# Trading the two row tiles of TensorE: one runs the first matmul of its tokens while the other runs output rounds

## The chip, the cores and the metric

One core of one Trainium2 chip. Times are device microseconds of whole executions; most executions of one kernel agree within 0.3%. A ratio is the mean time of one kernel's runs over that of the other's of the same rounds, so not quite the ratio of the medians that are quoted.

## The reference

A causal convolution of 7 taps per head (8 heads of 24 channels, weights through a softmax) over 32768 tokens of 192 channels, then a two-layer network with ELU between:

```python
out = einsum('hk,bskhg->bshg', softmax(weight), windows(x))     # 192 channels
h = out @ w_in                                                  # 192 -> 2048
g = where(h > 0, h, exp(min(h, 0)) - 1)
return g @ w_out                                                # 2048 -> 192
```

## The kernel before

The contraction of each matmul is 64 rows long, so TensorE works as two **row tiles** of 64 rows. Tokens come in super-tiles of 1024, and each tile has one **group** of 512 tokens for the first matmul. A **step** n is one slice of 128 of the 2048 hidden columns, for both groups:

- PE: three matmuls of 512 columns per tile (64 channels each) into one of three PSUM **slots** `H`, each slot with one bank per group.
- ACT: `E = exp(H)`, one instruction per group. POOL: clamps `E` to at most 1. DVE: `gT = max(E - 1, H)`. Only when DVE has read `H` is the slot free.
- PE again, one super-tile later: the second matmul. A **round** is one matmul of 192 columns on each tile. 64 rounds make one output **half** in the accumulator `ops` (two banks, one only for each group), and ACT copies it to `osb`. After 32 rounds the two tiles swap banks.

Eight steps belong to one output half. I number them 0 to 7: steps 0 to 6 hold 10, 10, 6, 6, 10, 11, 11 rounds, step 7 none, so that the copy of the accumulator has time. In step 5 a convolution of a later super-tile runs too, in two parts; it takes one slot as well, and ACT copies it to `csb`.

```python
HALF_STEPS = (10, 10, 6, 6, 10, 11, 11)
...
# PE: one step = the pair of groups, then its rounds (with convolution parts in between in step 5)
elif item[0] == "h":
    ...
    wait_slot(k)                              # s_tt >= 2*was+2: DVE is done with both groups
    for j in range(3):
        for r in range(2):                    # tile 0, tile 1
            ins = pe.matmul(H[:, k % 3, GS*r : GS*(r+1)], w_in[...], att[...],
                            start=(j == 0), stop=(j == 2), tile_position=(HP * r, 0))
    ins.then_inc(s_h)                         # one count for both groups
else:
    _, t, half, r0, r1 = item
    if r0 == 0: W(s_oev, 2 * t + half)        # the copy of the half before must be done
    for r in range(r0, r1):
        ...
        for rt in range(2):
            g = rt ^ second                   # banks swap after 32 rounds
            ins = pe.matmul(acc[:, g, D*kb : D*(kb+1)], gT[...], w_out[...],
                            tile_position=(HP * rt, 0))
    if r1 == NR: ins.then_inc(s_mm2)

# ACT, in the same order of items
if item[0] == "c": ...  W(s_cv, 2*m + 2);  csb <- H            # convolution's copy
elif item[0] == "h": W(s_h, n + 1); ...    E <- exp(H), twice  # both groups
else: if r1 == NR: evac(t, half)                               # osb <- ops, 128x768
```

Of the kernel before, what the change touches and what calls it, by code (L numbers as in the profile page):

```python
# [12 lines left out]
P = 128  # L13
HP = 64
FC = 128
D = 192
# [19 lines left out]
HALF_STEPS = (10, 10, 6, 6, 10, 11, 11)  # L36
# [8 lines left out]
def bass_lightweight_conv__then__act_elu_kernel(  # L45
# [26 lines left out]
    steps = []  # L72
# [9 lines left out]
    order = []  # L82
    last_half = (NS - 1, 1)
# [13 lines left out]
    for t in range(NS):  # L97
        base = NQ * (t + 1) + LAG
        for half in range(2):
            r = 0  # L100
            for i, cnt in enumerate(HALF_STEPS):
                rounds_at[base + 8 * half + i] = (t, half, r, r + cnt)
                r += cnt
            assert r == NR
    for n in range(NP + NQ + LAG):
# [8 lines left out]
        convs = [(k, u) for k, u in convs if k < NS]  # L114
        if n in rounds_at:
            t, half, r0, r1 = rounds_at[n]
            if (t, half) == last_half and r0 == 0:
                last_slot = take_slot(None)
            cuts = (r0, r0 + 3, r0 + 7, r1) if convs else (r0, r1)
            for part, (a, b) in enumerate(zip(cuts, cuts[1:])):  # L120
                order.append(("o", t, half, a, b))
                for k, u in convs:
                    if part < 2:
                        conv_at(k, u, part)
        else:
            for k, u in convs:
                for part in range(2):
                    conv_at(k, u, part)

# [3 lines left out]
    with ExitStack() as stack:  # L133
# [110 lines left out]
        def transpose(eng, W, s):  # L244
# [3 lines left out]
            if s >= 2:  # L248
                W(s_h, NQ * (s - 1))
# [6 lines left out]
        def _gpsimd(g: bass.BassGpSimd):  # L256
# [56 lines left out]
            for n in range(NP):  # L313
# [12 lines left out]
                for u in range(2):  # L326
                    W(s_exp, 2 * n + u + 1)
# [10 lines left out]
        def _scalar(a):  # L338
# [26 lines left out]
            for item in order:  # L365
# [6 lines left out]
                elif item[0] == "h":  # L372
                    n = item[1]
                    k = slot_of_pair[n] % 3
                    W(s_h, n + 1)
                    W(s_tt, 2 * (n - NE) + 2)
                    for u in range(2):
                        a.activation(  # L378
                            E[:, n % NE, u, :], H[:, k, GS * u : GS * (u + 1)], ACT.Exp
                        ).then_inc(s_exp)  # L380
# [6 lines left out]
        def _vector(v):  # L387
# [27 lines left out]
            for n in range(NP):  # L415
# [3 lines left out]
                for u in range(2):  # L419
                    W(s_clp, 2 * n + u + 1)  # L420
# [17 lines left out]
        def _tensor(pe):  # L438
            W = Waits(pe)

            def wait_slot(k):
# [3 lines left out]
                if was[0] == "h":  # L445
                    W(s_tt, 2 * was[1] + 2)
# [8 lines left out]
            warm(WARM[0])  # L455
            for item in order:
                if item[0] == "c":
                    _, m, part = item
                    s, u = divmod(m, 2)
                    k = slot_of_conv[m]  # L460
# [9 lines left out]
                    else:  # L470
                        if 2 <= m <= 3:
                            warm(WARM[2])
                        W(s_cswap, 2 * m + 2)

                    for q in range(2):
                        for rt in range(2):
                            hq = 2 * (rt ^ part) + q
                            h = HU * u + hq
                            rows = slice(HP * rt, HP + (KW - HP) * rt)
                            ins = pe.matmul(  # L480
                                H[0:CW, k % 3, 256 * hq : 256 * hq + UC],
                                Tm[rows, h, :] if s else Tk[rows, :, h],
                                xg[rows, s % NXB, :, CPH * h : CPH * (h + 1)].rearrange(
                                    "p w (j i) -> p j w i", j=3
                                ),
                                start=(part == 0 and q == 0),
                                stop=(part == 1 and q == 1),
                                tile_position=(HP * rt, 0),
                            )
                            if q == 1 and part == 0:  # L490
                                ins.then_inc(s_cswap)
                            elif q == 1:
                                ins.then_inc(s_cv)
                elif item[0] == "h":
                    n = item[1]
                    s, q = divmod(n, NQ)
                    if n == 0:
                        warm(WARM[1])
                    elif n < NQ - 1:
                        warm(WARM[2])  # L500
                    W(s_w[q // QA], 48)
                    W(s_wdp if q < QA else s_wd[1], 16)
                    W(s_att[s % 2], 16 * (s // 2 + 1))
                    k = slot_of_pair[n]
                    wait_slot(k)
                    for j in range(3):
                        for r in range(2):
                            ins = pe.matmul(  # L508
                                H[:, k % 3, GS * r : GS * (r + 1)],
                                w_in[HP * r : HP * (r + 1), j, FC * q : FC * (q + 1)],  # L510
                                att[HP * r : HP * (r + 1), s % 2, j, 0:GS],
                                start=(j == 0),
                                stop=(j == 2),
                                tile_position=(HP * r, 0),
                            )
                    ins.then_inc(s_h)
                else:
                    _, t, half, r0, r1 = item
                    W(s_w[2], 16)
                    if (t, half) == last_half:  # L520
                        acc = H[:, last_slot % 3, :].rearrange("p (g t) -> p g t", g=2)
                        if r0 == 0:
                            wait_slot(last_slot)
                    else:
                        acc = ops
                        if r0 == 0:
                            W(s_oev, 2 * t + half)
                    for r in range(r0, r1):

                        second, (q, kb) = r // (NR // 2), divmod(r % (NR // 2), 2)  # L530
                        W(s_tt, 2 * (NQ * t + q) + 2)
                        if second:
                            W(s_swap, 2 * (2 * t + half + 1))
                        t0 = 2 * P * half + P * kb
                        for rt in range(2):
                            g = rt ^ second
                            ins = pe.matmul(  # L537
                                acc[:, g, D * kb : D * (kb + 1)],
                                gT[HP * rt : HP * (rt + 1), t % NG3, q, g, t0 : t0 + P],
                                w_out[HP * rt : HP * (rt + 1), q, :],  # L540
                                start=(r == 0),
                                stop=(r == NR - 1),
                                tile_position=(HP * rt, 0),
                            )
                            if r == NR // 2 - 1:
                                ins.then_inc(s_swap)
                    if r1 == NR:
                        ins.then_inc(s_mm2)
# [79 lines left out]
```

## Time and profile before

Before: 758.62 us median of 4 runs (757.49 to 760.06).

The page of the kernel before: busy time and share of the span by engine, then the chain that ended last.

```profile
PE 746.0 (99%) x11872; PEld 510.7 (68%) x11872; DVE 636.0 (84%) x1033; ACT 645.8 (85%) x1155; POOL 668.3 (88%) x1110
...
PE 94%; DVE 2%; DMA 2%; POOL 1%; ACT 1%; issue 0%; SPq 0%
```

PE is never idle for long. Start to start in the trace, two first matmuls side by side take 216 ns, a round 82.5 ns, two convolution matmuls 102.5 ns. One half is then 24 x 216 + 64 x 82.5 + 4 x 102.5 ns = 10.87 us of TensorE work; the trace repeats every 11.19 us. So 0.32 us per half, 20 us in the run, are stalls.

The timeline of PE in the kernel before, around the end of one half (start, length in us, group, count): step 5 with its convolution, step 6 (0.82 + 1.07), then the pairs of steps 7 and 0 as one group of 12, then the first rounds of the next half.

```profile
402.84 0.53 PE L537 MATMUL ops<-w_out,gT 64*128 64x192 f16 x8
403.19 0.82 PE L508 MATMUL H<-att,w_in 64*128 64x512 bf16 x6
403.85 1.07 PE L537 MATMUL ops<-w_out,gT 64*128 64x192 f16 x22
404.75 1.46 PE L508 MATMUL H<-att,w_in 64*128 64x512 bf16 x12
406.05 0.99 PE L537 MATMUL ops<-w_out,gT 64*128 64x192 f16 x20
```

ACT in the same stretch:

```profile
403.07 0.97 ACT L371 ACTIVATE csb<-H 112x960 bf16<-112x960 f32 x1
404.05 1.09 ACT L378 ACTIVATE E<-H 128x512 f32<-128x512 f32 x2
405.02 0.82 ACT L359 ACTIVATE osb<-ops 128x768 f32<-128x768 f32 x1
405.71 3.10 ACT L378 ACTIVATE E<-H 128x512 f32<-128x512 f32 x6
```

Read the two together: the last round of the half ends near 404.9, the copy runs from 405.02 to 405.84, and PE wants the accumulator again at 406.05. The twelve matmuls between (1.3 us) hide the copy, with 0.2 us to spare.

### The profile page before, as it was taken

How to read it: one execution, taken by the hardware profiler on the slowest of the kernel's cores; microseconds unless marked ns; L12 is line 12 of the kernel's file. 1: busy time of each engine (PE TensorE's matmuls, PEld its weight loads, DVE VectorE, ACT ScalarE, POOL GpSimd, SP SyncE). 2: the span in 40 equal slices, each digit the busy share in tenths (PEclk: the TensorE clock that was granted, in tenths of full speed). 3: DMA queues.
4: the chain of work that ended last, by engine and by line, in shares of the span. 5: the costliest groups of instructions: out<-in, count | busy, mean ns of one | idle time of the engine just before them, and what ended most of it. 6: DMA issues, size and time to landing. Idle time of an engine off the chain costs nothing.

```text
span 756.5 us, 27972 instructions
## 1 busy us (share of the span) xinstructions
PE 746.0 (99%) x11872; PEld 510.7 (68%) x11872; DVE 636.0 (84%) x1033; ACT 645.8 (85%) x1155; POOL 668.3 (88%) x1110
## 2 busy tenths in 40 slices
PE   8999999999999999999999999999999999999997
PEld 3246776776767676676677667677767667767676
DVE  2588898889889889889889888988988988988993
ACT  1589989988998998998998988899899899899882
POOL 3799999999999999999999999999999999998882
PEclk9999999999999999999999999999999999999999
DMA  5855535445534524554533553542464453353212
GB/s 99 127 68 92 86 65 93 53 76 93 92 62 91 89 48 85 94 76 75 93 55 74 93 91 60 92 85 47 90 93 70 82 92 53 77 93 79 46 45 64
DMA packets 135501, 59.34 MB, mean 78 GB/s; under 512 B 101680, under 2 KB 134576, under 8 KB 135376
## 3 DMA queue, kind: packets, MB, share of 16 engines
q0 software_dynamic: 44992, 17.67, 22.2%
q1 hardware_dynamic: 90112, 39.68, 21.7%
q8 instruction: 93, 1.52, 0.9%
q14 instruction: 32, 0.26, 0.1%
q10 hardware_dynamic: 272, 0.20, 0.1%
HBM read 34.80 MB, written 25.45 MB: 80 GB/s over the span
## 4 chain that ended last, share of the span: by engine, by line
PE 94%; DVE 2%; DMA 2%; POOL 1%; ACT 1%; issue 0%; SPq 0%
PE H L508 45%; PE ops L537 43%; PE H L480 4%; DVE gT L421 1%; PE ops L453 1%; POOL E L328 1%; PE H L537 1%; DMA conv_band<-wprb 1%; ACT E L378 0%; DMA Tk<-conv_band 0%; DMA wq<-in_weight_dram 0%; POOL xg L275 0%; POOL w_out L316 0%; ACT osb L359 0%; DVE osb L432 0%
## 5 line engine op out<-in xcount | busy, mean ns | idle before, releaser
L421 DVE SCALAR_TENSOR_TENSOR gT<-E,H 128x512 f16<-128x512 f32 x1024 | 630.4, 682 | 94.2 <-POOL E L328 86.4
L328 POOL TENSOR_SCALAR E<-E 128x512 f32<-128x512 f32 x1024 | 604.9, 614 | 61.6 <-ACT E L378 54.2
L378 ACT ACTIVATE E<-H 128x512 f32<-128x512 f32 x1024 | 546.2, 604 | 80.9 <-PE H L508 65.0
L537 PE MATMUL ops<-w_out,gT 64*128 64x192 f16 x8064 | 426.0, 243 | 0.9 <-DVE gT L421 0.9
L537 PEld LDWEIGHTS ops<-w_out,gT 64*128 64x128 f16 x8064 | 352.2, 94 | 104.1 <-ACT osb L359 10.7
L508 PE MATMUL H<-att,w_in 64*128 64x512 bf16 x3072 | 408.0, 378 | 1.3 <-DVE gT L421 1.2
L508 PEld LDWEIGHTS H<-att,w_in 64*128 64x128 bf16 x3072 | 127.1, 94 | 108.2 <-DVE gT L421 5.5
L371 ACT ACTIVATE csb<-H 112x960 bf16<-112x960 f32 x63 | 61.2, 971 | 14.1 <-PE H L480 12.0
L275 POOL DMA_DIRECT2D xg<-in_x_dram x65 | 59.3, 913 | 6.3 <-DVE csb L411 6.1
L359 ACT ACTIVATE osb<-ops 128x768 f32<-128x768 f32 x63 | 51.5, 817 | 5.1 <-PE ops L537 5.1
L480 PE MATMUL H<-xg,Tm 64*112 64x240 bf16 x496 | 49.6, 272 | 1.0 <-DVE gT L421 0.6
L480 PEld LDWEIGHTS H<-xg,Tm 64*112 64x112 bf16 x496 | 26.0, 126 | 10.2 <-issue 3.3
L453 PE MATMUL ops<-zw 128*128 128x512 bf16 x96 | 26.8, 417 | 1.5 <-DVE zw L389 1.5
L453 PEld LDWEIGHTS ops<-zw 128*128 128x128 bf16 x96 | 8.6, 105 | 16.5 <-issue 9.6
L411 DVE CAST csb<-H 112x960 bf16<-112x960 f32 x1 | 1.2, 1157 | 10.5 <-PE H L480 10.5
L432 DVE COPY osb<-H 128x384 f32<-128x384 f32 x1 | 0.6, 557 | 8.9 <-PE H L537 8.9
L537 PE MATMUL H<-w_out,gT 64*128 64x192 f16 x128 | 5.6, 243 | 0.1
L537 PEld LDWEIGHTS H<-w_out,gT 64*128 64x128 f16 x128 | 5.2, 94 | 0.3 <-PE H L537 0.3
L307 POOL DMA_DIRECT2D w_in<-w_in x1 | 0.7, 682 | 5.3 <-DMA w_in<-in_moe_w_in_dram 5.3
L351 ACT ACTIVATE osb<-H 128x384 f32<-128x384 f32 x1 | 0.5, 491 | 4.7 <-PE H L537 4.7
L293 POOL DMA_DIRECT2D w_in<-in_moe_w_in_dram x6 | 3.5, 598 | 0.9 <-DMA att<-csb 0.9
L480 PE MATMUL H<-xg,Tk 64*112 64x240 bf16 (+1 forms) x16 | 2.0, 406 | 2.1 <-DMA Tk<-conv_band 2.1
(20 smaller groups left out, 12.0 us busy)
## 6 DMA issues: line engine op xcount, KB each, us to landing
out_dram<-osb SPq DMA_DIRECT2D x127, 192.0 KB, 3.5
xg<-in_x_dram POOLq DMA_DIRECT2D x62, 240.0 KB, 4.9
w_in<-in_moe_w_in_dram POOLq DMA_DIRECT2D x6, 128.0 KB, 5.2
w_out<-in_moe_w_out_dram POOLq DMA_DIRECT2D x1, 768.0 KB, 7.8
att<-csb SPq DMA_TRANSPOSE x32, 6.2
xg<-in_x_dram POOLq DMA_DIRECT2D x2, 192.0 KB, 4.4
w_in<-w_in POOLq DMA_DIRECT2D x1, 384.0 KB, 5.1
w_in<-w_in SPq DMA_DIRECT2D x1, 384.0 KB, 4.7
```

What stands on the lines that cost most here:

```text
L275: g.dma_start(xg[0:rows, b, 2 * w0 + gr : 2 * w1 : 2, :], src).then_inc(s_x[b][gr], 16)
L293: g.dma_start(w_in[0:HP, j, c0:c1], bass.AP(tensor=moe_w_in.tensor, offset=8 * j * FF + c0, ap=[[CPH * FF, HEADS], [FF, 8], [1, c1 - c0]], ...
L328: g.tensor_scalar(out=E[:, n % NE, u, :], in0=E[:, n % NE, u, :], scalar1=1.0, scalar2=0.0, op0=ALU.min, op1=ALU.max,).then_inc(s_clp)
L359: a.activation(osb[:, b, :, :, :].rearrange("p g k d -> p g (k d)"), ops[:, :, 0 : 2 * D], ACT.Copy,).then_inc(s_oev)
L371: a.activation(*conv_evac(W, m), ACT.Copy).then_inc(s_ce)
L378: a.activation(E[:, n % NE, u, :], H[:, k, GS * u : GS * (u + 1)], ACT.Exp).then_inc(s_exp)
L411: v.tensor_copy(*conv_evac(W, 1)).then_inc(s_cd)
L421: v.scalar_tensor_tensor(out=gT[:, s % NG3, q, u, :], in0=E[:, n % NE, u, :], scalar=1.0, in1=H[:, slot_of_pair[n] % 3, GS * u : GS * (u + ...
L453: pe.matmul(ops[:, 0, :], zw[:, 0:P], zw[:, 0:GS], start=True, stop=True)
L480: ins = pe.matmul(H[0:CW, k % 3, 256 * hq : 256 * hq + UC], Tm[rows, h, :] if s else Tk[rows, :, h], xg[rows, s % NXB, :, CPH * h : CPH * ...
L508: ins = pe.matmul(H[:, k % 3, GS * r : GS * (r + 1)], w_in[HP * r : HP * (r + 1), j, FC * q : FC * (q + 1)], att[HP * r : HP * (r + 1), s ...
L537: ins = pe.matmul(acc[:, g, D * kb : D * (kb + 1)], gT[HP * rt : HP * (rt + 1), t % NG3, q, g, t0 : t0 + P], w_out[HP * rt : HP * (rt + 1) ...
```

## The change

Its intent: let one tile run its three long matmuls while the other runs rounds, then trade, and hand on `H` per group. Each group then reaches ACT by itself, and PE waits for half a slot only. The cost of each matmul is written into the program (`MM_H`, `MM_O`, `MM_C`), and the two tiles' instructions are merged by these clocks. The tile that begins with its long matmuls is tile 0 in the first 32 rounds and tile 1 in the last 32 (`lead`). The core of the diff:

```diff
-HALF_STEPS = (10, 10, 6, 6, 10, 11, 11)
+HALF_STEPS = (9, 9, 7, 7, 10, 11, 11)
+MM_H, MM_O, MM_C = 216.0, 82.5, 102.5
+    def lead(n):
+        return int(n in rounds_at and rounds_at[n][2] >= NR // 2)
 # ACT, POOL, DVE: one wait and one count per group, the leading group first
-                    W(s_h, n + 1)
-                    for u in range(2):
+                    for at, u in enumerate((lead(n), 1 - lead(n))):
+                        W(s_h, 2 * n + at + 1)
 # PE: half a slot is enough
-                    W(s_tt, 2 * was[1] + 2)
+                    W(s_tt, 2 * was[1] + (1 if u == lead(was[1]) else 2))
 # PE: (cut) the two tiles' lists, merged by their clocks
+                    if convs:
+                        early = 5 if rt != first else 0
+                        lists[rt] = rounds[rt][:early] + convs[0][rt] + ... + convs[1][rt] + ...
+                lists[first] = pair[first] + lists[first]
+                lists[1 - first] = lists[1 - first] + pair[1 - first]
+                emit(lists, first)
```

More of the change, by code (lines that the diff above doesn't have):

```diff
@@ L1 @@
+import itertools
 from contextlib import ExitStack
@@ L69, in bass_lightweight_conv__then__act_elu_kernel @@
     x_flat = x.rearrange("b s d -> (b s) d")
-    steps = []
     slot_of_pair, slot_of_conv, prior = {}, {}, []
@@ L82, in bass_lightweight_conv__then__act_elu_kernel @@
     order = []
+    steps = []
     last_half = (NS - 1, 1)
@@ L103, in bass_lightweight_conv__then__act_elu_kernel @@
                 r += cnt
-            assert r == NR
+            assert r == NR and NR // 2 in itertools.accumulate(HALF_STEPS)
+    def lead(n):
+        return int(n in rounds_at and rounds_at[n][2] >= NR // 2)
     for n in range(NP + NQ + LAG):
@@ L114, in bass_lightweight_conv__then__act_elu_kernel @@
         convs = [(k, u) for k, u in convs if k < NS]
+        first = len(order) - (n < NP)
         if n in rounds_at:
@@ L118, in bass_lightweight_conv__then__act_elu_kernel @@
                 last_slot = take_slot(None)
-            cuts = (r0, r0 + 3, r0 + 7, r1) if convs else (r0, r1)
+            cuts = (r0, r0 + 3, r0 + 8, r1) if convs else (r0, r1)
             for part, (a, b) in enumerate(zip(cuts, cuts[1:])):
@@ L128, in bass_lightweight_conv__then__act_elu_kernel @@
                     conv_at(k, u, part)
+        steps.append((n, first, len(order)))
     band = nc.dram_tensor("conv_band", (P, TW, HEADS), BF16).ap()
@@ L248, in transpose @@
             if s >= 2:
-                W(s_h, NQ * (s - 1))
+                W(s_h, 2 * NQ * (s - 1))
             eng.dma_start_transpose(
@@ L325, in _gpsimd @@
                     batch_zeros(s + 2)
-                for u in range(2):
-                    W(s_exp, 2 * n + u + 1)
+                for at, u in enumerate((lead(n), 1 - lead(n))):
+                    W(s_exp, 2 * n + at + 1)
                     g.tensor_scalar(
@@ L374, in _scalar @@
                     k = slot_of_pair[n] % 3
-                    W(s_h, n + 1)
                     W(s_tt, 2 * (n - NE) + 2)
-                    for u in range(2):
+                    for at, u in enumerate((lead(n), 1 - lead(n))):
+                        W(s_h, 2 * n + at + 1)
                         a.activation(
@@ L418, in _vector @@
                     W(s_mm2, 2 * (s - NG3 + 1))
-                for u in range(2):
-                    W(s_clp, 2 * n + u + 1)
+                for at, u in enumerate((lead(n), 1 - lead(n))):
+                    W(s_clp, 2 * n + at + 1)
                     v.scalar_tensor_tensor(
@@ L439, in _tensor, with wait_slot @@
             W = Waits(pe)
-            def wait_slot(k):
+            def wait_slot(k, u=None):
                 was = prior[k]
@@ L453, in warm, with free, conv_items, ready @@
                     pe.matmul(ops[:, 0, :], zw[:, 0:P], zw[:, 0:GS], start=True, stop=True)
-            warm(WARM[0])
-            for item in order:
-                if item[0] == "c":
-                    _, m, part = item
-                    s, u = divmod(m, 2)
-                    k = slot_of_conv[m]
+            half_done, halves = {}, {}
+            def free():
+                return True
+            def conv_items(m, part):
+                s, u = divmod(m, 2)
+                k = slot_of_conv[m]
+                def ready():
                     if part == 0:
@@ L470, in _tensor @@
                     else:
-                        if 2 <= m <= 3:
-                            warm(WARM[2])
                         W(s_cswap, 2 * m + 2)
-                    for q in range(2):
-                        for rt in range(2):
-                            hq = 2 * (rt ^ part) + q
-                            h = HU * u + hq
-                            rows = slice(HP * rt, HP + (KW - HP) * rt)
-                            ins = pe.matmul(
-                                H[0:CW, k % 3, 256 * hq : 256 * hq + UC],
-                                Tm[rows, h, :] if s else Tk[rows, :, h],
-                                xg[rows, s % NXB, :, CPH * h : CPH * (h + 1)].rearrange(
-                                    "p w (j i) -> p j w i", j=3
-                                ),
-                                start=(part == 0 and q == 0),
-                                stop=(part == 1 and q == 1),
-                                tile_position=(HP * rt, 0),
-                            )
-                            if q == 1 and part == 0:
-                                ins.then_inc(s_cswap)
-                            elif q == 1:
-                                ins.then_inc(s_cv)
-                elif item[0] == "h":
-                    n = item[1]
-                    s, q = divmod(n, NQ)
-                    if n == 0:
-                        warm(WARM[1])
-                    elif n < NQ - 1:
-                        warm(WARM[2])
-                    W(s_w[q // QA], 48)
-                    W(s_wdp if q < QA else s_wd[1], 16)
-                    W(s_att[s % 2], 16 * (s // 2 + 1))
-                    k = slot_of_pair[n]
-                    wait_slot(k)
-                    for j in range(3):
-                        for r in range(2):
-                            ins = pe.matmul(
-                                H[:, k % 3, GS * r : GS * (r + 1)],
-                                w_in[HP * r : HP * (r + 1), j, FC * q : FC * (q + 1)],
-                                att[HP * r : HP * (r + 1), s % 2, j, 0:GS],
-                                start=(j == 0),
-                                stop=(j == 2),
-                                tile_position=(HP * r, 0),
-                            )
-                    ins.then_inc(s_h)
-                else:
-                    _, t, half, r0, r1 = item
-                    W(s_w[2], 16)
-                    if (t, half) == last_half:
-                        acc = H[:, last_slot % 3, :].rearrange("p (g t) -> p g t", g=2)
-                        if r0 == 0:
-                            wait_slot(last_slot)
-                    else:
-                        acc = ops
-                        if r0 == 0:
-                            W(s_oev, 2 * t + half)
-                    for r in range(r0, r1):
-                        second, (q, kb) = r // (NR // 2), divmod(r % (NR // 2), 2)
-                        W(s_tt, 2 * (NQ * t + q) + 2)
-                        if second:
-                            W(s_swap, 2 * (2 * t + half + 1))
-                        t0 = 2 * P * half + P * kb
-                        for rt in range(2):
-                            g = rt ^ second
-                            ins = pe.matmul(
-                                acc[:, g, D * kb : D * (kb + 1)],
-                                gT[HP * rt : HP * (rt + 1), t % NG3, q, g, t0 : t0 + P],
-                                w_out[HP * rt : HP * (rt + 1), q, :],
-                                start=(r == 0),
-                                stop=(r == NR - 1),
-                                tile_position=(HP * rt, 0),
-                            )
-                            if r == NR // 2 - 1:
-                                ins.then_inc(s_swap)
-                    if r1 == NR:
-                        ins.then_inc(s_mm2)
@@ new lines, in matmul @@
+                def matmul(rt, q):
+                    ready()
+                    hq = 2 * (rt ^ part) + q
+                    h = HU * u + hq
+                    rows = slice(HP * rt, HP + (KW - HP) * rt)
+                    ins = pe.matmul(
+                        H[0:CW, k % 3, 256 * hq : 256 * hq + UC],
+                        Tm[rows, h, :] if s else Tk[rows, :, h],
+                        xg[rows, s % NXB, :, CPH * h : CPH * (h + 1)].rearrange(
+                            "p w (j i) -> p j w i", j=3
+                        ),
+                        start=(part == 0 and q == 0),
+                        stop=(part == 1 and q == 1),
+                        tile_position=(HP * rt, 0),
+                    )
+                    if q == 1:
+                        ins.then_inc(s_cv if part else s_cswap)
+                        halves[m, part] = halves.get((m, part), 0) + 1
@@ new lines, in gate, with pair_items, matmul @@
+                def gate():
+                    return part == 0 or halves.get((m, 0)) == 2
+                return [
+                    [(MM_C, lambda rt=rt, q=q: matmul(rt, q), gate) for q in range(2)]
+                    for rt in range(2)
+                ]
+            def pair_items(n):
+                s, q = divmod(n, NQ)
+                k = slot_of_pair[n]
+                def matmul(r, j):
+                    if j == 0:
+                        W(s_w[q // QA], 48)
+                        W(s_wdp if q < QA else s_wd[1], 16)
+                        W(s_att[s % 2], 16 * (s // 2 + 1))
+                        wait_slot(k, r)
+                    ins = pe.matmul(
+                        H[:, k % 3, GS * r : GS * (r + 1)],
+                        w_in[HP * r : HP * (r + 1), j, FC * q : FC * (q + 1)],
+                        att[HP * r : HP * (r + 1), s % 2, j, 0:GS],
+                        start=(j == 0),
+                        stop=(j == 2),
+                        tile_position=(HP * r, 0),
+                    )
+                    if j == 2:
+                        at = int(r != lead(n))
+                        assert len(units) == 2 * n + at
+                        units.append((n, r))
+                        ins.then_inc(s_h)
+                return [
+                    [(MM_H, lambda r=r, j=j: matmul(r, j), free) for j in range(3)]
+                    for r in range(2)
+                ]
@@ new lines, in round_items, with matmul @@
+            def round_items(t, half, r0, r1):
+                last = (t, half) == last_half
+                acc = H[:, last_slot % 3, :].rearrange("p (g t) -> p g t", g=2) if last else ops
+                def matmul(rt, r):
+                    W(s_w[2], 16)
+                    if r == 0 and last:
+                        wait_slot(last_slot)
+                    elif r == 0:
+                        W(s_oev, 2 * t + half)
+                    second, (q, kb) = r // (NR // 2), divmod(r % (NR // 2), 2)
+                    W(s_tt, 2 * (NQ * t + q) + 2)
+                    if second:
+                        W(s_swap, 2 * (2 * t + half + 1))
+                    t0 = 2 * P * half + P * kb
+                    g = rt ^ second
+                    ins = pe.matmul(
+                        acc[:, g, D * kb : D * (kb + 1)],
+                        gT[HP * rt : HP * (rt + 1), t % NG3, q, g, t0 : t0 + P],
+                        w_out[HP * rt : HP * (rt + 1), q, :],
+                        start=(r == 0),
+                        stop=(r == NR - 1),
+                        tile_position=(HP * rt, 0),
+                    )
+                    if r == NR // 2 - 1:
+                        ins.then_inc(s_swap)
+                    if r == NR - 1:
+                        half_done[t, half] = half_done.get((t, half), 0) + 1
+                        if half_done[t, half] == 2:
+                            ins.then_inc(s_mm2)
+                return [
+                    [(MM_O, lambda rt=rt, r=r: matmul(rt, r), free) for r in range(r0, r1)]
+                    for rt in range(2)
+                ]
@@ new lines, in _tensor, with emit @@
+            units = []
+            clock = [0.0, 0.0]
+            def emit(lists, first):
+                at = [0, 0]
+                while any(at[rt] < len(lists[rt]) for rt in range(2)):
+                    rt = min(
+                        (rt for rt in range(2) if at[rt] < len(lists[rt]) and lists[rt][at[rt]][2]()),
+                        key=lambda rt: (clock[rt], rt != first),
+                    )
+                    took, issue, _ = lists[rt][at[rt]]
+                    at[rt] += 1
+                    issue()
+                    clock[rt] += took
@@ new lines, in level @@
+            def level():
+                clock[:] = [max(clock)] * 2
+            warm(WARM[0])
+            for part in range(2):
+                for u in range(2):
+                    emit(conv_items(u, part), 0)
+            for n, i0, i1 in steps:
+                items = order[i0:i1]
+                first = lead(n)
+                pair = pair_items(n) if n < NP else [[], []]
+                if n == 0:
+                    warm(WARM[1])
+                elif n < NQ - 1:
+                    warm(WARM[2])
+                if n not in rounds_at:
+                    level()
+                    emit(pair, first)
+                    for item in items:
+                        if item[0] == "c":
+                            if item[2] and 2 <= item[1] <= 3:
+                                warm(WARM[2])
+                            level()
+                            emit(conv_items(*item[1:]), first)
+                    continue
+                t, half, r0, r1 = rounds_at[n]
+                rounds = round_items(t, half, r0, r1)
+                convs = [conv_items(*item[1:]) for item in items if item[0] == "c"]
+                lists = [[], []]
+                for rt in range(2):
+                    if convs:
+                        early = 5 if rt != first else 0
+                        lists[rt] = (
+                            rounds[rt][:early]
+                            + convs[0][rt]
+                            + rounds[rt][early : early + 6]
+                            + convs[1][rt]
+                            + rounds[rt][early + 6 :]
+                        )
+                    else:
+                        lists[rt] = rounds[rt]
+                lists[first] = pair[first] + lists[first]
+                lists[1 - first] = lists[1 - first] + pair[1 - first]
+                emit(lists, first)
```

## The prediction

> **What bounds it now.** TensorE. The page: PE 99% busy, the chain that ended last 94% PE, clock 0.997. Start-to-start in the trace: a round of two output matmuls (one per tile) 82.5 ns, a pair of first matmuls 216 ns, a pair of convolution matmuls about 102.5 ns. One super-tile is 48 x 216 + 128 x 82.5 + 8 x 102.5 ns = 21.75 us; the timeline's period is 22.38 us. So all PE stalls are about 0.63 us per super-tile, 20 us in the run: that is all that can be won, since both tiles already run together at full rate.
>
> **What the stalls are.** In the short steps (6 rounds) the period is 1196 ns against 1143 of work: the PSUM slot comes back late. Latencies from the timeline: end of H matmuls to ACT 201 ns, ACT start to POOL start 677, POOL to DVE 711, DVE to PE 738: 2.33 us, plus 495 for the second group. Handing on per group, with 7 rounds there, should remove them: up to -20 us.
>
> **What it adds.** Matmuls keep program order, so one tile's wait stops both (the Trainium skill, "TensorE: Matmul & The Clock Gate", Part 2, step 1: only weight loads are pulled ahead; the trace agrees, loads lead by one round). Two waits move onto the path, once per output half (8 steps):
>
> 1. Output accumulator. Before, two whole first-matmul groups (1.30 us) separate the last round of a half from the first round of the next; the copy to osb (817 ns) just fits. After, tile 1's last round ends with its step, one 648 ns group follows, and tile 1 then starts with round 0 at once. The copy alone needs 201+817+58 ns. Worse, ACT works in order, and the exponential of tile 0's late H comes ahead of the copy: at least 0.9 us stall.
>
> 2. Convolution. Its slot was that of the pair two steps before, whose second group now ends only at the end of its step; tile 0 asks after 5 rounds: 1473+412 = 1885 ns later, against 2.33 us: stall about 0.46 us. ACT also holds the convolution's copy until that step's late exponential, which pushes the accumulator's copy back further.
>
> The loop for one half, from round 0 to the next round 0: steps 1 to 5 6703 + conv stall 460 + conv step 1965, then on ACT 201 + 640 (exponential) + 980 (conv copy) + 495 + 477 (two exponentials) + 817 (copy) + 58 = 12.80 us. Before: 11.19 us. So +1.61 us in 59 halves, about +0.45 in three without convolution: +96 us.
>
> **Predicted: 854 us, 815 to 880.** Faster by over 2%: 0.02; within 2%: 0.03; slower: 0.95.
>
> **What would show it.** Period of a super-tile near 25.6 us; PE waiting about 60 times for ACT's osb copy, 0.6 to 1.5 us each; PE waiting for DVE gT before each convolution, about 0.45 us, and before the roundless step; PE share of the chain down, ACT's up; ACT busy under 80%. Within steps the tiles keep 216 and 82.5 ns, and the short-step slot stalls are gone.
>
> **What would make it wrong.** If tiles at different matmul lengths do not overlap at full rate (the skill's "TensorEngine Tiling (Array Packing)", Key Properties, calls tiles independent; this trace shows only equal lengths side by side), slower still. If ACT reaches the copy earlier than in my loop, only the 0.9 us stall remains, about 800 us.

## The result and the profile after

After: 839.37 us median of 4 runs (838.05 to 840.64), against 758.62. The ratio is 1.1055 (95% interval 1.103 to 1.108; the four and four runs listed alone give 1.106): 10.6% slower. The granted clock is 0.998 to 1.0 in the four runs, so the clock is not the cause.

The page of the kernel after, the same lines:

```profile
PE 786.7 (94%) x11869; PEld 633.1 (76%) x11872; DVE 661.9 (79%) x1033; ACT 671.2 (80%) x1155; POOL 678.5 (81%) x1110
...
PE 66%; ACT 15%; issue 10%; DVE 4%; POOL 3%; DMA 2%; POOLq 0%; SPq 0%; ACTq 0%
```

Every engine but PEld (68% to 76%) got less busy in share, and the chain now passes through ACT for 15% of the span. PE still shows 94%, although a half now takes 12.52 us for the same 10.87 us of work (87%): a tile that works alone counts as a busy PE.

The chain of waits: who waited for whom, us in total, times, longest. First the two largest lines of this kind in the kernel before, both on the weight loads:

```profile
PEld ops L537 <- ACT osb L359: 10.7, 62, 0.2
PEld H L508 <- DVE gT L421: 5.5, 10, 1.2
```

The same and a new one in the kernel after. PE and its weight loads (PEld) are listed apart, and one stall can show in both, so they are not added.

```profile
PEld H L522 <- DVE gT L429: 52.8, 73, 0.8
PEld ops L557 <- ACT osb L367: 36.2, 62, 0.7
PE H L522 <- DVE gT L429: 32.9, 60, 0.6
PEld ops L557 <- PE ops L557: 21.7, 62, 0.4
```

All come about once per half (there are 64). `H <- DVE gT` is a slot that is not free, `ops <- ACT osb` the accumulator's copy, and `ops <- PE ops`, which is new, the bank swap. PE at the end of a half in the kernel after (the first two lines are the end of step 6):

```profile
419.19 0.38 PE L522 MATMUL H<-att,w_in 64*128 64x512 bf16 x1
419.23 0.32 PE L557 MATMUL ops<-w_out,gT 64*128 64x192 f16 x2
420.12 1.03 PE L522 MATMUL H<-att,w_in 64*128 64x512 bf16 x7 [0.55 <-DVE gT L429]
421.24 0.25 PE L557 MATMUL ops<-w_out,gT 64*128 64x192 f16 x1
421.25 0.39 PE L522 MATMUL H<-att,w_in 64*128 64x512 bf16 x1
421.33 0.33 PE L557 MATMUL ops<-w_out,gT 64*128 64x192 f16 x2
```

and ACT in the same stretch:

```profile
416.77 0.60 ACT L386 ACTIVATE E<-H 128x512 f32<-128x512 f32 x1 [0.31 <-PE H L522]
418.05 0.60 ACT L386 ACTIVATE E<-H 128x512 f32<-128x512 f32 x1 [0.68 <-PE H L522]
418.54 0.96 ACT L379 ACTIVATE csb<-H 112x960 bf16<-112x960 f32 x1
419.39 1.09 ACT L386 ACTIVATE E<-H 128x512 f32<-128x512 f32 x2
420.35 0.83 ACT L367 ACTIVATE osb<-ops 128x768 f32<-128x768 f32 x1
```

Set these beside the lines of before. ACT sat idle for 0.68 us until 418.05 for the late group of step 5, whose long matmuls now come last in their step. Only then, in its own order, could it do the convolution's copy, two exponentials and the accumulator's copy, which began at 420.35 although the last round had started near 419.3. PE meanwhile met two waits: step 7's slot, held by the late group of step 5 (until 420.12), and round 0 of the next half, which waits for the copy (until 421.24). The seventh of the seven matmuls at 420.12 is tile 0's first of step 0; its second one started at 421.247, just after round 0 (421.237), although nothing of its own held it back: in the merged program it stands behind round 0 of tile 1, so the wait at round 0 held both tiles. The Trainium skill says that matmuls keep program order and only weight loads are pulled ahead ("TensorE: Matmul & The Clock Gate", Part 2, step 1); the trace of the kernel before agrees, but in this one the starts of the matmuls do not. By the merge's clocks rounds 1 and 2 of tile 1 (82.5 and 165) also stand ahead of that second long matmul (216), yet they started after it, at 421.329 and 421.412. One tile's wait stopped the other, but past the wait the two tiles' matmuls did not start in the program's order.

One half of the trace after, from round 0 at 408.684 to round 0 at 421.237 (12.55 us), against the start that each step would have had right after the work before it:

| where PE stopped | waits for | us |
|---|---|---|
| step 4, first round after the bank swap | the count of its own tile's last round | 0.26 |
| step 5, convolution part 1 | DVE, late group of step 3 | 0.21 |
| step 7, its pair | DVE, late group of step 5 | 0.73 |
| step 0, round 0 | ACT's copy of the accumulator | 0.47 |
| work | | 10.87 |
| sum | | 12.54 |

The first row needs a closer look. Round 31 of tile 0 started at 413.637 and its modelled end is 413.880, but its semaphore count, the signal that round 32 waits for, came only at 414.141. In the program the last long matmul of tile 1's step 3 stands ahead of round 31; in the trace it started after it (413.709, modelled end 414.085) and was counted at 414.099. In 62 of 63 halves looked at, the count of tile 0's round 31 follows that of the long matmul ahead of it by 42 to 43 ns, and all 1472 counts of TensorE's matmuls in the run come in program order (taken from the program built from kernel.py), although the starts do not. In the kernel before, the later of the swap's two counts comes 0.287 us after its round began; here 0.505 us (medians). So the stall is not the time that the round takes: its count comes behind that of a longer matmul of the other tile. No run was made that moves only this.

And where the tiles only trade, they do so at full speed: step 1 of this half (9 rounds) lasts from 410.084 to 411.474, 1.39 us, which is 9 x 82.5 + 3 x 216 ns. The Trainium skill calls tiles independent ("TensorEngine Tiling (Array Packing)", Key Properties); the kernel before had shown that for equal lengths only, and this trace agrees for 512 columns beside 192.

### The profile page after: what moved, and what is told of

It reads as the page before. It is cut to its first block, busy times and chain, and to the rows that moved or that the text cites. A ratio compares the mean times of both kernels' runs of the same rounds, so it can differ in the third digit from the quotient of the medians.

```text
span 836.1 us, 27969 instructions
## 1 busy us (share of the span) xinstructions
PE 786.7 (94%) x11869; PEld 633.1 (76%) x11872; DVE 661.9 (79%) x1033; ACT 671.2 (80%) x1155; POOL 678.5 (81%) x1110
## 4 chain that ended last, share of the span: by engine, by line
PE 66%; ACT 15%; issue 10%; DVE 4%; POOL 3%; DMA 2%; POOLq 0%; SPq 0%; ACTq 0%
PE ops L557 36%; PE H L522 24%; ACT E L386 9%; ACT osb L367 5%; PE H L490 5%; DVE gT L429 3%; POOL E L336 3%; PE H L557 1%; ACT csb L379 1%; DMA conv_band<-wprb 1%; DMA att<-csb 0%; PE ops L461 0%; DMA wq<-in_weight_dram 0%; DMA Tk<-conv_band 0%; POOL w_in L301 0%
## 5 line engine op out<-in xcount | busy, mean ns | idle before, releaser
L429 DVE SCALAR_TENSOR_TENSOR gT<-E,H 128x512 f16<-128x512 f32 x1024 | 656.3, 685 | 148.9 <-POOL E L336 134.1
L336 POOL TENSOR_SCALAR E<-E 128x512 f32<-128x512 f32 x1024 | 614.9, 615 | 131.9 <-ACT E L386 124.6
L522 PE MATMUL H<-att,w_in 64*128 64x512 bf16 x3072 | 666.0, 377 | 32.9 <-DVE gT L429 32.9
L386 ACT ACTIVATE E<-H 128x512 f32<-128x512 f32 x1024 | 585.3, 605 | 138.3 <-PE H L522 115.2
L557 PE MATMUL ops<-w_out,gT 64*128 64x192 f16 x8064 | 629.2, 243 | 6.8 <-ACT osb L367 1.3
L557 PEld LDWEIGHTS ops<-w_out,gT 64*128 64x128 f16 x8064 | 543.9, 94 | 86.1 <-ACT osb L367 36.2
L522 PEld LDWEIGHTS H<-att,w_in 64*128 64x128 bf16 x3072 | 253.7, 94 | 78.6 <-DVE gT L429 52.8
L490 PE MATMUL H<-xg,Tm 64*112 64x240 bf16 x496 | 71.7, 267 | 3.4 <-DVE gT L429 2.4
L490 PEld LDWEIGHTS H<-xg,Tm 64*112 64x112 bf16 x496 | 42.7, 127 | 17.1 <-issue 9.7
L490 PEld LDWEIGHTS H<-xg,Tk 64*112 64x112 bf16 (+1 forms) x16 | 1.7, 297 | 1.1 <-DMA Tk<-conv_band 1.1
```

The lines of the kernel that those rows point to most:

```text
L336: g.tensor_scalar(out=E[:, n % NE, u, :], in0=E[:, n % NE, u, :], scalar1=1.0, scalar2=0.0, op0=ALU.min, op1=ALU.max,).then_inc(s_clp)
L386: a.activation(E[:, n % NE, u, :], H[:, k, GS * u : GS * (u + 1)], ACT.Exp).then_inc(s_exp)
L429: v.scalar_tensor_tensor(out=gT[:, s % NG3, q, u, :], in0=E[:, n % NE, u, :], scalar=1.0, in1=H[:, slot_of_pair[n] % 3, GS * u : GS * (u + ...
L490: ins = pe.matmul(H[0:CW, k % 3, 256 * hq : 256 * hq + UC], Tm[rows, h, :] if s else Tk[rows, :, h], xg[rows, s % NXB, :, CPH * h : CPH * ...
L522: ins = pe.matmul(H[:, k % 3, GS * r : GS * (r + 1)], w_in[HP * r : HP * (r + 1), j, FC * q : FC * (q + 1)], att[HP * r : HP * (r + 1), s ...
L557: ins = pe.matmul(acc[:, g, D * kb : D * (kb + 1)], gT[HP * rt : HP * (rt + 1), t % NG3, q, g, t0 : t0 + P], w_out[HP * rt : HP * (rt + 1) ...
```

## The experiments

My theory: the loss is the four waits of the table, which come from where the late groups, the swap, the convolution and round 0 meet. Rival A: handing on per group costs time (twice the semaphore counts and waits). Rival B: the mixing itself slows TensorE. Rival C: the new step sizes do. "Together" below means that a step runs both tiles' long matmuls first and then its rounds, as before. Halves are half of the median period of a super-tile in the trace. The kernel before ran again beside each set (medians 758.3 to 759.3).

| run | edit | us, median | ratio to before | half, us |
|---|---|---|---|---|
| before | | 758.62 | 1 | 11.19 |
| after | | 839.37 | 1.1055 | 12.52 |
| tog_all | after, all steps together | 759.1 | 1.001 | 11.20 |
| tog_5 | step 5 together | 811.18 | 1.0688 | 12.06 |
| tog_06 | steps 0 and 6 together | 824.58 | 1.0858 | 12.29 |
| tog_056 | steps 0, 5, 6 together | 772.32 | 1.019 | 11.41 |
| tog_0456 | steps 0, 4, 5, 6 together | 758.57 | 1.0007 | 11.19 |
| b_steps | before with 9,9,7,7 | 758.81 | 1.0008 | 11.20 |
| copy_first | after, ACT reordered | 849.41 | 1.1185 | 12.66 |
| both_first | after, ACT reordered twice | 851.53 | 1.1219 | 12.72 |
| tog_5_copy_first | tog_5 and copy_first | 818.86 | 1.0786 | 12.18 |
| mix123_8888 | tog_0456, other sizes | 762.63 | 1.0054 | 11.27 |
| tog_all_8888 | tog_all, the same sizes | 771.22 | 1.0164 | 11.41 |
| half_copy | tog_0456, half the copy (wrong result) | 753.95 | 0.9942 | 11.12 |

### Taking the mixing out, step by step

The edit of the five "together" kernels is one branch ahead of the merge, and the list of steps:

```diff
+TOGETHER = (0, 5, 6)                      # tog_056; other lists in the others
+                if step_of[n] in TOGETHER:
+                    level(); emit(pair, first); level()
+                    ... rounds of both tiles, convolution parts after 3 and 8 of them ...
+                    continue
```

**tog_all.** 

> The change with no step mixed: every step runs the first matmuls of both tiles together and then its rounds, as before; the per-group semaphores and the 9,9,7,7 steps stay. My theory (the loss is two waits that only the mixing puts on the path): 745 to 758 us, the loss is gone. Rival A (handing on per group, with more semaphore counts and waits, costs the time): stays near 835 us. Rival B (tiles at different matmul lengths slow each other) also expects about 750 here.

Measured 759.1 us, ratio 1.001 (0.9995 to 1.0025). Rival A is out: all of the per-group handing on is still there, and the loss is gone. It also wins nothing by itself.

**b_steps.** The first edit of the diff alone, put into the kernel before. 

> The kernel before with only the step sizes of the change (9,9,7,7 in place of 10,10,6,6). The short steps then hold 1225 ns of TensorE work against the 1196 ns that two groups take on DVE. I expect a little faster, 748 to 758 us; if step sizes were part of the loss (rival C), above 770 us.

Measured 758.81 us, ratio 1.0008 (0.9993 to 1.0023). Rival C is out. So is the small gain that I expected; see below.

**tog_056.** 

> Mixed only in steps 1 to 4 of each half; the step before and after the accumulator's copy (6 and 0) and the convolution's step (5) are together as before. My theory: no conv stall, no stall on the accumulator's copy, only the wait at the group swap (0.26 us per half, seen in the trace after) is left: half 11.13 us, about 752 us (745 to 762). Rival B (mixing itself slows TensorE, in proportion to the mixed steps): 4 of 7 steps are still mixed, so about 800 us.

Measured 772.32 us. Four of seven steps are mixed and the loss is 2%, not 5%: Rival B is out in the form that it was given. My number was 20 us too low: the waits of PE show a second slot wait in each half, at step 6, whose slot was that of the still mixed step 4 with its late group (the weight loads idle 0.30 and 0.36 us there in two halves of the trace). From start to start PE loses 0.11 to 0.17 us there, so this wait is about half of the 0.28 us by which the half is longer than expected; the rest is spread over steps 0 and 5:

```profile
PEld H L524 <- DVE gT L431: 31.3, 121, 0.5
```

**tog_0456.** 

> Mixed only in steps 1, 2 and 3; so the group swap, the convolution and the accumulator's copy all have a first-matmul group of both tiles ahead of them. My theory: the swap wait goes too, and the short-step slot stalls of the kernel before are gone: half about 10.9 us, 738 to 748 us, faster than before. Rival B: about 785 us.

Measured 758.57 us, ratio 1.0007 (0.9991 to 1.0024). With step 4 together too, the rest of the loss goes: on balance the three steps that still trade cost nothing. But the gain over the kernel before did not come.

**tog_5.** 

> The change, but the convolution's step (5) together. Its slot then is asked for 0.9 us into the step in place of 0.41, and its copy on ACT no longer waits for a late exponential. My theory: the conv stall goes (0.2 us), the roundless step's slot wait goes, and the wait for the accumulator's copy stays at about 0.9 us: half about 12.06 us, about 808 us (800 to 818). If the convolution were the main loss: below 780 us.

Measured 811.18 us, as expected; a half took 12.06 us, the expected number. The waits on the weight loads show what went (the slot wait fell from 52.8 us to 12.1) and what stayed and grew, the wait for the copy:

```profile
PEld ops L559 <- ACT osb L369: 63.1, 62, 1.0
PEld ops L559 <- PE ops L559: 21.8, 62, 0.4
PEld H L524 <- DVE gT L431: 12.1, 61, 0.5
```

**tog_06.** 

> The change, but the two steps around the accumulator's copy (6 and 0) run both tiles' first matmuls together and then the rounds. Steps 1 to 5 stay mixed. My theory, from the intervals of the trace after: round 0 now has two first-matmul groups ahead of it, but the roundless step still waits for the slot of the convolution step, whose late group ends with its step; half about 12.1 us in place of 12.53, about 810 us (800 to 820). If the copy alone were the loss: about 780 us. If mixing itself were: about 815 us, with unchanged times of the mixed steps.

Measured 824.58 us. PE's waits no longer list the accumulator's copy, but the slot wait of step 7 is still there:

```profile
PEld H L524 <- DVE gT L431: 49.5, 74, 0.8
```

The direction is as expected, the size 14 us above and outside the stated range. The time alone does not speak for my theory (810) against a loss by the mixing itself (815); the waits and the next runs do. The two parts are not additive: tog_5 alone wins 28 us, tog_06 alone 15, both together 67. Each wait hides part of the other: in tog_5, with most of the slot wait gone, the copy's grew from 36.2 to 63.1 us. The likely reason, not tested alone, is that both end at work that ACT does in one order.

### Leaving PE alone and moving ACT's copies

**copy_first.** TensorE's order is that of the change; only ACT's is edited:

```diff
 for at, u in enumerate((lead(n), 1 - lead(n))):
+    for late in between.get(n, []) if at == 1 else []:   # step 6: evac of this half (cut)
+        evac(late[1], late[2])
     W(s_h, 2 * n + at + 1)
```

> The change with one thing moved on ACT: in step 6 the accumulator's copy goes ahead of the exponential of the late group. TensorE's order is untouched. My theory: the copy starts one exponential (0.48 us) sooner and round 0 follows, until the roundless step's own slot wait binds: half shorter by 0.45 us, about 811 us. A rival in which TensorE is slowed by the mixing, not by ACT's order, expects no change (837 us).

Measured 849.41 us: 10 us slower than the change, where I expected 28 us faster. The expected part did happen. In the waits of the weight loads the accumulator's copy all but went (36.2 us in the change, 0.9 now), and the ACT timeline shows the copy right after the first exponential of step 6:

```profile
422.78 0.96 ACT L375 ACTIVATE csb<-H 112x960 bf16<-112x960 f32 x1
423.63 0.60 ACT L407 ACTIVATE E<-H 128x512 f32<-128x512 f32 x1
424.11 0.82 ACT L367 ACTIVATE osb<-ops 128x768 f32<-128x768 f32 x1
424.80 1.59 ACT L407 ACTIVATE E<-H 128x512 f32<-128x512 f32 x3
```

But the slot wait now comes 121 times in place of 60, twice per half:

```profile
PE H L543 <- DVE gT L450: 55.0, 121, 0.6
PEld ops L578 <- ACT osb L367: 0.9, 3, 0.3
```

The second one is at step 1 (414.24 in place of 413.77 in one half of the trace). Step 1 takes the slot of step 6, and the late exponential of step 6 is the one that the copy had overtaken. My expectation had left that slot out. So a change of ACT's order alone moves PE's stalls, with no edit to TensorE's order: a second point against Rival B, and a failure of my "28 us".

**both_first.** As above, with the convolution's copy ahead of the late exponential of step 5 too. 

> As copy_first, and in step 5 the convolution's copy also goes ahead of the late exponential. ACT alone would then reach the accumulator's copy 0.69 us sooner than in the change, but the late exponential of step 5 comes 0.43 us later, and with it the slot for which the roundless step waits; so round 0 can start no earlier than in the change but for a few hundredths. My theory with both waits: about 835 us, worse than copy_first. If ACT's copy were the only wait: about 796 us.

Measured 851.53 us, against 849.41 for copy_first. The intervals of the two ratios overlap (1.120 to 1.1237 and 1.1163 to 1.1206), so the expected order is not clear of noise, and the level is wrong by 16 us. The reason is not the one just given: PE now waits once per half, for step 7's slot (60.6 us in 64 waits, the longest 1.0), and no longer for the copy (0.9 us). That is the exchange that I expected, but the half came out at 12.72 us in place of about 12.5; where the last 0.2 us come from stays open.

**tog_5_copy_first.** With the coupling known, the same edit on tog_5, where the copy was the only large wait. 

> tog_5 (convolution's step together; there the only large wait left is the 1.0 us for the accumulator's copy) with the copy moved ahead of step 6's late exponential. Round 0 starts 0.48 us sooner; but the late exponential then follows 0.69 us after the copy began, and step 1's slot is the one it frees, 2.1 us later: about 0.5 us of wait at step 1, which copy_first showed. My theory of two coupled waits: about 811 us, as tog_5. If the copy's wait were the only one: about 782 us.

Measured 818.86 us. That speaks for two coupled waits (811 us) and against the single one (782 us), though it is 8 us slower than tog_5, where I expected the same time. The expected wait appeared, in addition to what is left of the other:

```profile
PEld ops L580 <- ACT osb L369: 35.6, 62, 0.6
PE H L545 <- DVE gT L452: 24.0, 62, 0.4
```

### Where the expected gain went

The prediction counted 20 us of stalls in the kernel before as winnable. Four kernels with different orders (before, b_steps, tog_all, tog_0456) all take 758 to 759 us. Their traces show where PE loses time, from start to start, in medians over the halves. In the kernel before it is 0.05 to 0.06 us ahead of each of steps 2, 3 and 4 and 0.14 us in step 5, 0.32 in all. In b_steps the losses ahead of steps 3 and 4 are gone, but ahead of step 2, which takes the slot of the last step 7, it is now 0.17 to 0.22 us. In tog_0456 those ahead of steps 2 and 3 are gone, but ahead of step 4 it is 0.14 to 0.15 us. The sums stay at 0.29 to 0.34 us. So the short-step stalls were removed as planned, and others took their place. Three runs ask why.

**mix123_8888** and **tog_all_8888.** `HALF_STEPS = (8, 8, 8, 8, 10, 12, 10)`, with steps 1, 2, 3 mixed, and with none.

> Mixed only in steps 1, 2 and 3 of each half (as tog_0456), with steps of 8,8,8,8,10,12,10 rounds. In tog_0456 TensorE still waited for DVE gT at step 4 (0.2 us: steps 2 and 3 are 2.45 us long, one group handed on takes 2.33 us and the queue on POOL) and at step 6 (4th and 5th sizes sum to 21). With 8 rounds in each, steps 2 and 3 are 2.62 us, and 10+12 rounds cover step 6. My theory: almost no stall is left, half 10.9 to 11.0 us, 738 to 748 us, faster than both kernels. If a limit outside of TensorE's order (POOL or ACT work) fixes the half at 11.19 us, as the four equal times near 758 us might mean: 758 us again.

> The same step sizes with no step mixed. The roundless step's slot comes back about 3.0 us after its groups end (it waits behind the accumulator's copy on ACT), and two steps of 8 rounds last 2.62 us: a stall of about 0.4 us at step 2. My theory: half about 11.2 to 11.3 us, 758 to 765 us, so the step sizes alone do not win what the mixed steps win. Rival (the sizes alone make the difference): 738 to 748 us here too.

Measured 762.63 and 771.22 us. Neither number was met: the first is slower than the kernel before, by 0.5%. What the pair does show is that trading three steps is worth 1.1% where the step sizes leave PE waiting for slots: 771.22 to 762.63 us with the same sizes. The gain that the change was meant to bring exists, but only against a worse baseline.

**half_copy.** A wrong result:

```diff
-                    osb[:, b, :, :, :].rearrange("p g k d -> p g (k d)"),
-                    ops[:, :, 0 : 2 * D],
+                    osb[:, b, :, 0, :],
+                    ops[:, :, 0:D],
```

(and `osb` set to zero at the start). 

> Wrong result on purpose: tog_0456, but ACT copies only half of the accumulator (128x384 in place of 128x768), so that the copy takes about 0.49 us (as the one copy of that size in the trace) in place of 0.82. Why: four kernels with quite different stalls (before, b_steps, tog_all, tog_0456) all take 758 us, so something outside of TensorE's order sets a half's 11.19 us. Theory L: a loop through ACT, from the last round through the accumulator's copy, the exponentials queued behind it, POOL (which then runs without a gap for six pairs), DVE and the slots back to TensorE; it shortens by what the copy shortens, 0.2 to 0.3 us a half: 740 to 746 us. Rival M: the sum of POOL's own work sets it: no change, 757 to 760 us.

The copy's mean time is now 498 ns in place of 817. Measured 753.95 us, ratio 0.9942 (0.9924 to 0.9959), a half of 11.12 us against 11.19. Neither theory's number is met. The copy took 0.32 us less per half, and 0.07 us of it arrived (11.19 to 11.12, against tog_0456, which differs by this edit alone). So the copy's length is part of what sets the half, as a loop through it would have it, and POOL's sum of work is not all of it: POOL's clamps kept their length (613 ns in place of 614). PE's remaining waits in this run are for DVE's `gT`, small and spread. What holds these kernels near 758 us stays open.

## Why the prediction was right

**The size and the sign.** 854 us predicted, 815 to 880 given, 839.4 measured: +81 us against +96.

**"so both tiles already run together at full rate."** Right, and it leaves nothing to be won by overlapping more: a mixed step costs what a step together costs (1.39 us for 9 rounds).

**"Matmuls keep program order, so one tile's wait stops both."** The conclusion held where it mattered (tile 0 stood until 421.247 behind tile 1's round 0). The premise held in part: counts came in program order, starts did not, and that cost the swap stall, which the prediction did not have.

**Wait 1, the accumulator.** Right in cause. The prediction put all of it at round 0 (0.6 to 1.5 us) and mentioned the roundless step only as a wait to be seen. In the trace it is split: 0.73 us at step 7's slot, then 0.47 us at round 0. tog_5 and tog_06 each remove one of the two, and the other takes over in part.

**Wait 2, the convolution.** 0.46 us predicted. The trace has 0.21 us there, and 0.26 us at the bank swap one step earlier, which the prediction did not have. That the sum is right is not luck alone: the convolution waits for DVE's work on step 3, which began before the swap, so a stall at the swap makes the convolution's own wait shorter. The swap stall is itself a product of the change. Before, the swap came after a pair of long matmuls of both tiles; now tile 0 goes from round 31 to round 32 with nothing between, and the count of its round 31 comes late, behind a long matmul of tile 1.

**The loop of 12.80 us.** This is the term that was mis-sized: the half is 12.52 us. Two intervals of ACT were read from the trace before as if they were its own cost. "640 (exponential)" was the time from an exponential to the convolution's copy, and "980 (conv copy)" the time from that copy to the next exponential. In the kernel before, both ended at something from PE: the copy started 37 ns after the last convolution matmul's end (403.035), the exponential 38 ns after the pair's last matmul's end (404.014). After, where ACT is the one that is waited for, they measure 0.49 us (418.05 to 418.54) and 0.85 us (418.54 to 419.39). The difference is 0.28 us per half, in 59 halves 16 us, and the prediction was 15 us too high.

**What was to be seen.** Super-tile period near 25.6 us: 25.04. ACT's copy waited for about 60 times: 62. ACT busy under 80%: 80.3%, just missed. PE's share of the chain down and ACT's up: 94% to 66%, 1% to 15%. Short-step slot stalls gone: steps 2 and 3 (7 rounds) take 1.225 us each, exactly their work. PE's wait for the copy was to be 0.6 to 1.5 us each time; it is 0.47 in the table.

**"up to -20 us."** Not shown in any run. With the harmful meetings taken out (tog_0456), the time was that of the kernel before: a stall that was removed in one step came back in another. No version beat the kernel before with a correct result.

## What to carry to other kernels

A share of 99% on one engine does not say that the stalls left on it can be won one by one: find the loop that each belongs to before counting it as a gain. When one instruction stream drives two tiles, moving work to the end of a step delays everything that is queued behind that work's result on the other engines; look at which in-order engine gets it late, and what else that engine owes. A wait for a short matmul can last as long as a longer one ahead of it on the other tile: here 0.505 us from its start to its count in place of 0.287. And take an interval from a trace as an engine's cost only where that engine was the one being waited for; here two intervals that contained someone else's wait made up the whole error in the length of a half.

## What the Trainium skill lacked or had wrong

- "TensorE: Matmul & The Clock Gate", Part 3, says that matmuls keep program order in start and end. Here the starts do not, where the tiles' matmuls differ in length: in step 0 tile 0's second long matmul starts at 421.247, ahead of rounds 1 and 2 of tile 1 (421.329 and 421.412), which stand before it in the program. The counts do: all 1472 come in program order. (Ends of matmuls are modelled in this profile.) The page has no figure for tiles of different lengths side by side; here a mixed step of 9 rounds takes 1.39 us, the plain sum of one tile's work.
- "ScalarE: Activation LUTs", section "What ACT_TABLE_LOAD costs", gives an overlap of about 93 ns for back-to-back activations. Here exponentials of 128x512 with a mean of 604 ns follow one another after 477 to 495 ns, and an exponential follows the 817 ns copy after 691 ns: an overlap of 100 to 130 ns.
- No page has the cost of counts in program order when a short matmul of one tile follows a long one of the other: here a round's count comes 0.505 us after its start in place of 0.287, which is a stall of 0.26 us per half at the bank swap, where a tile waits for that count.
